# Leaving out TensorE weight loads whose tile the array already holds

## The chip, the cores and the metric

The kernel runs on one core of one Trainium2 chip. The metric is the device time of one execution in microseconds (us), lower is better. Most executions of one kernel agree within 0.3%; a change counts as faster or slower from 2% on.

## The reference

Four residual layers on an input of 2048 tokens by 1024 features in bf16: linear attention (A), gated MLP (B), A, B, each behind a layer norm. Cut to its arithmetic:

```python
def _A_ref(x, wqkv, wo):                       # 32 heads of 32
    q, k, v = split(x @ wqkv)
    pq, pk = phi(q), phi(k)                    # phi(t) = (t+1 if t>0 else exp(t)) + 1e-6
    kv = einsum("bhsd,bhse->bhde", pk, v);  z = sum_s(pk)
    o = (pq @ kv) / (pq . z + 1e-6)
    return o @ wo
def _B_ref(x, w_gate, w_up, w_down):           # F = 3584
    return ((x @ w_gate) * (x @ w_up)) @ w_down

x = x + _A_ref(ln(x)); x = x + _B_ref(ln(x)); x = x + _A_ref(ln(x)); x = x + _B_ref(ln(x))
```

## The kernel before

TensorE does nearly everything: its matmuls are busy 98% of the span. In the program a matmul names a stationary tile (128x128, the "weights" of the array, whether they come from a weight matrix or from activations) and the columns that go through it, 128 to 512 in this kernel. Each matmul is preceded by its own load of the stationary tile: the trace has 7,663 loads, all of 128x128. Two forms matter here.

The first is the helper for outputs of 1024 columns. It makes two matmuls of 512 columns with the **same** stationary tile, so every second load fetches a tile that is already there. The K, Q, G, M and output products of attention use it, and so does the down projection of the MLP:

```python
def both(ps, lhsT, rhs, start, stop):
    for n in range(2):
        nc.tensor.matmul(out=ps[:, n, :], lhsT=lhsT, rhs=rhs[:, n * NB:(n + 1) * NB], start=start, stop=stop)   # L205
...
def d_unit(t, last):                           # down projection of token tile t
    ...
    for f in range(KF):                        # KF = 28
        both(ps, hT[:, f, tl * P:(tl + 1) * P], wd[f], f == 0, f == KF - 1)
```

The second has a **new** stationary tile for every matmul: gate and up, and the small KV products of 128 columns:

```python
def gu_unit(i, f):
    ...
    for n in range(2):
        w = ring[(2 * i + n) % 6]
        for k in range(KD):                    # KD = 8
            nc.tensor.matmul(out=ps[:, n, :], lhsT=w[:, k, j * P:(j + 1) * P], rhs=xT[g % 2][:, k, :], ...)     # L437
def kv_unit(m):
    ...
    for c in range(KD):
        nc.tensor.matmul(out=acc[0][:, c, :], lhsT=wkv[:, m, c * P:(c + 1) * P],
                         rhs=Gs[m % 2][:, c * P:(c + 1) * P], ...)                                              # L295
```

The last token tile of the program (L464) has three passes of 512, 256 and 256 columns, again with a new tile each time.

## Time and profile before

| | before |
|---|---|
| time, median of the first 3 runs | 1659.09 us |
| span in the profile, granted TensorE clock | 1657.2 us, 0.995 of full |
| TensorE matmuls busy (PE) | 1627.2 us, 98% |
| weight loads (PEld), on a row of their own | 744.8 us, 45%, 7,663 loads |

The first lines of the page give the busy time of each engine with its share of the span and its instruction count:

```profile
span 1657.2 us, 17618 instructions
...
PE 1627.2 (98%) x7512; PEld 744.8 (45%) x7663; DVE 607.9 (37%) x889; ACT 286.3 (17%) x384; POOL 54.0 (3%) x141
...
q8 instruction: 60, 0.98, 0.2%
```

A busy share does not tell what limits TensorE, since records of neighbouring matmuls overlap: one of 512 columns lasts 379 ns but the next starts long before it ends. The *spacing* tells it. It is read in the chain of work that ended last, in order of time (columns: start in us, length in us, engine, output tile and line, number of matmuls). First the gate/up stage, then the down stage, then a KV product between two attention products:

```profile
272.53 10.74 PE ps L437 x49
283.27 0.05 issue
283.32 10.74 PE ps L437 x49
...
358.87 10.74 PE ps L205 x49
...
369.66 10.74 PE ps L205 x49
...
988.79 0.45 PE kv L295 x8
```

One matmul record in 50 is lost (gate/up has 3,513 matmul records beside 3,584 loads), which is why the pieces break; the 0.05 us is not a stall. A piece steps 10.79 us for 50 matmuls, 215.8 ns each, in both stages. In the last token tile a matmul of 512 columns steps 215.7 ns and one of 256 steps 109.3 ns, so 256 columns take 106.4 ns and 512 about 213 ns. The KV products step 0.45 us / 8 = 56 ns, each with a new tile. So TensorE streams columns almost without a break, and the 98 ns that a load record lasts lies beside the matmuls.

### The profile page before, as it was taken

To read this page: it belongs to the slowest core of one execution; us is meant where nothing else is said; L and a number is where in the kernel's file an instruction comes from. 1 tells how busy PE (TensorE), PEld (TensorE's weight loads), DVE (VectorE), ACT (ScalarE), POOL (GpSimd) and SP (SyncE) were. 2 spreads that over 40 slices of the span, in tenths; PEclk is the share of its full clock that TensorE was granted. 3 is DMA by queue.
4 is the path that set the end of the run, shared out by engine and by line. 5 is a ranking of instruction groups with operands and counts; after the bars stand their busy time and mean duration, and the time that the engine had idled before them with its cause. 6 is when DMAs were issued, how large, how long until landed. Compare 5 with 4: busy or idle time off the path is not lost.

```text
span 1657.2 us, 17618 instructions
## 1 busy us (share of the span) xinstructions
PE 1627.2 (98%) x7512; PEld 744.8 (45%) x7663; DVE 607.9 (37%) x889; ACT 286.3 (17%) x384; POOL 54.0 (3%) x141
## 2 busy tenths in 40 slices
PE   8989999999999999999999999999999999999999
PEld 3434444444444444444444444444444444444444
DVE  5797782311321231143345687532113113211111
ACT  4532301100110110011035322011001101100110
POOL 1100000000000000010000000000000000000000
PEclk9999999999999999999999999999999999999999
DMA  6322683630551363043420247555215504521400
GB/s 209 64 64 47 183 247 115 177 115 1 171 159 51 90 175 118 0 153 102 77 76 1 70 96 225 158 156 165 84 64 151 179 26 143 167 84 64 153 0 26
DMA packets 234686, 182.56 MB, mean 110 GB/s; under 512 B 100080, under 2 KB 215408, under 8 KB 234608
## 3 DMA queue, kind: packets, MB, share of 16 engines
q1 hardware_dynamic: 234608, 181.43, 37.5%
q8 instruction: 60, 0.98, 0.2%
q14 instruction: 18, 0.15, 0.0%
HBM read 153.09 MB, written 4.19 MB: 95 GB/s over the span
## 4 chain that ended last, share of the span: by engine, by line
PE 90%; DVE 7%; issue 1%; DMA 1%; POOL 1%; ACT 0%; SPq 0%; DVEq 0%; ACTq 0%
PE ps L437 46%; PE ps L205 42%; DVE GL L252 1%; DVE st L182 1%; PE ps L464 1%; DVE R L213 1%; DVE X L320 0%; DVE den L272 0%; DVE PQ L276 0%; PE kv L295 0%; POOL rstd L190 0%; DVE PQ L213 0%; DVE tmp L270 0%; DVE e L212 0%; DVE R L195 0%
## 5 line engine op out<-in xcount | busy, mean ns | idle before, releaser
L437 PE MATMUL ps<-xT,R 128*128 128x512 bf16 x2380 | 525.8, 379 | 2.8
L437 PEld LDWEIGHTS <-R 128*128 128x128 bf16 x2432 | 238.0, 98 | 287.0
L441 DVE TENSOR_TENSOR R<-gs,ps 128x512 bf16<-128x512 f32 x224 | 153.8, 687 | 533.6 <-ACT gs L440 533.6
L205 PEld LDWEIGHTS <-R 128*128 128x128 bf16 x2248 | 220.4, 98 | 266.6 <-issue 3.1
L440 ACT COPY gs<-ps 128x512 f32<-128x512 f32 x224 | 131.3, 586 | 1044.5 <-PE ps L437 1021.6
L437 PE MATMUL ps<-xT,W 128*128 128x512 bf16 x1133 | 250.6, 379 | 1.0
L205 PEld LDWEIGHTS <-xT 128*128 128x128 bf16 x1536 | 149.8, 98 | 184.2 <-issue 5.3
L205 PE MATMUL ps<-W,xT 128*128 128x512 bf16 x999 | 225.1, 380 | 4.5 <-ACT xT L345 1.7
L437 PEld LDWEIGHTS <-W 128*128 128x128 bf16 x1152 | 112.7, 98 | 135.9
L205 PE MATMUL ps<-W,R 128*128 128x512 bf16 x729 | 169.6, 379 | 0.7
L445 DVE TENSOR_TENSOR X<-X,ps 128x1024 bf16<-128x1024 bf16 (+2 forms) x34 | 39.4, 1158 | 335.9 <-PE ps L205 315.2
L205 PE MATMUL ps<-R,R 128*128 128x512 bf16 x503 | 114.5, 383 | 0.6
L205 PE MATMUL ps<-PQ,R 128*128 128x512 bf16 x484 | 111.5, 379 | 0.6
L205 PE MATMUL ps<-R,xT 128*128 128x512 bf16 x502 | 110.8, 379 | 0.9 <-DVE X L320 0.4
L210 ACT ACTIVATE e<-ps 128x1024 bf16<-128x1024 f32 x56 | 57.4, 1024 | 152.1 <-PE ps L205 150.6
L182 DVE BATCH_NORM_STATS2 st<-X 128x6 f32<-128x512 bf16 x128 | 82.1, 681 | 2.0 <-DMA X<-in_A_x_dram 1.8
L188 POOL TENSOR_SCALAR ve<-mv 128x1 f32<-128x1 f32 x64 | 15.7, 245 | 1362.8 <-DVE mv L186 1362.8
L205 PE MATMUL ps<-xT,R 128*128 128x512 bf16 x243 | 58.2, 379 | 0.3
L205 PE MATMUL ps<-GL,R 128*128 128x512 bf16 x244 | 58.2, 379 | 0.2
L320 DVE TENSOR_TENSOR X<-X,ps 128x1024 bf16<-128x1024 bf16 x32 | 38.5, 1209 | 33.1 <-PE ps L205 30.9
L212 DVE TENSOR_SCALAR e<-e 128x1024 bf16<-128x1024 bf16 x64 | 27.2, 424 | 63.2 <-ACT e L210 63.2
L195 DVE TENSOR_SCALAR R<-X,mv,rstd 128x1024 bf16<-128x1024 bf16 x64 | 33.7, 543 | 36.0 <-POOL rstd L190 36.0
(55 smaller groups left out, 462.9 us busy)
## 6 DMA issues: line engine op xcount, KB each, us to landing
R<-in_B_w_gate_dram SPq DMA_DIRECT2D x38, 1024.0 KB, 5.4
R<-in_B_w_up_dram SPq DMA_DIRECT2D x38, 1024.0 KB, 7.4
W<-in_B_w_gate_dram SPq DMA_DIRECT2D x18, 1024.0 KB, 5.2
W<-in_B_w_up_dram SPq DMA_DIRECT2D x18, 1024.0 KB, 7.2
W<-in_A_wqkv_dram SPq DMA_DIRECT2D x10, 1024.0 KB, 6.8
W<-in_B_w_down_dram SPq DMA_DIRECT2D x6, 1024.0 KB, 11.3
PQ<-in_B_w_down_dram SPq DMA_DIRECT2D x4, 1024.0 KB, 7.9
X<-in_A_x_dram SPq DMA_DIRECT2D x15, 256.0 KB, 5.7
```

What stands on the lines that cost most here:

```text
L182: nc.vector.bn_stats(out=st[:, c, :], in_=X[:, t, c * NB:(c + 1) * NB])
L195: nc.vector.tensor_scalar(out=dst, in0=X[:, t, :], scalar1=mv[:, 0:1], scalar2=rstd[:], op0=ALU.subtract, op1=ALU.mult)
L205: nc.tensor.matmul(out=ps[:, n, :], lhsT=lhsT, rhs=rhs[:, n * NB:(n + 1) * NB], start=start, stop=stop)
L210: nc.scalar.activation(out=e[:], in_=flat(ps), func=ACT.Exp, **sc)
L212: nc.vector.tensor_scalar(out=e[:], in0=e[:], scalar1=1.0, scalar2=EPS, op0=ALU.min, op1=ALU.add)
L213: nc.vector.tensor_tensor(out=dst, in0=dst, in1=e[:], op=ALU.add)
L252: nc.vector.tensor_tensor(out=zacc, in0=in0, in1=PK[:, t, :], op=ALU.add)
L320: nc.vector.tensor_tensor(out=X[:, t, :], in0=X[:, t, :], in1=flat(ps), op=ALU.add)
L437: nc.tensor.matmul(out=ps[:, n, :], lhsT=w[:, k, j * P:(j + 1) * P], rhs=xT[g % 2][:, k, :], start=(k == 0), stop=(k == KD - 1))
L440: nc.scalar.copy(out=gs[:], in_=ps[:, 0, :])
L441: nc.vector.tensor_tensor(out=hT[:, f, :], in0=gs[:], in1=ps[:, 1, :], op=ALU.mult)
L445: nc.vector.tensor_tensor(out=X[:, t, a:b], in0=X[:, t, a:b], in1=ps, op=ALU.add)
```

## The change

The intent: where two loads of the same tile follow one another, the second is useless; leaving it out takes a quarter of all loads away from TensorE. The program is compiled first, so that loads and matmuls are separate instructions and their waits are known. Then each load that names the tile of the load before it, and that carries no wait and no signal, is dropped.

```diff
+    ctx.close()
+    tc.close()
+    tc.compile()
+    for block in nc.cur_f.blocks:
+        held, keep = None, []
+        for i in block.instructions:
+            if isinstance(i, mybir.InstLdweights):
+                w = str(i.ins[0])
+                if w == held and not i.has_wait() and not i.has_update():
+                    continue
+                held = w
+            keep.append(i)
+        if len(keep) < len(block.instructions):
+            block.instructions[:] = keep
```

## The prediction

> **What bounds the kernel now.** The page shows TensorE busy 98% of a 1657.2 us span, clock 0.995; the chain that ended last is 90% TensorE matmuls, 7% VectorE. Matmul records overlap (379 ns each), so the spacing decides. In the chain in order of time, dense stages are equal pieces: 49 recorded matmuls end after 10.74 us and the next piece starts 10.79 us after this one, that is 50 matmuls (one record in 50 is lost) at 215.8 ns. [...]TensorE streams at nearly its peak; only about 40 us of the span are stalls and small matmuls.
>
> **Are weight loads visible in that spacing?** The 7,663 recorded loads take 744.8 us (45%), 98 ns each by the groups, but on their own row, under the matmuls. Gate/up (L437) needs a new tile for every matmul, the down stage (L205) repeats every second one: same piece, same step. The KV products (L295) run 8 matmuls of 128 columns, each with its own new load, in 0.45 us: 56 ns each, so even there the loads hide. In the last token tile (L464) the timeline gives 215.7 ns per 512 columns and 109.3 ns per 256: about 2.5 ns above the columns whatever the width. [...]
>
> **What the change removes.** Loads whose tile is already held and that carry no wait or signal. From the code: every second load of the two-half helper (K, Q, G, M, output and down projection), 1,908, 3 of 4 in each z sum (6), and 9 in the warm-up: about 1,923 of some 7,790. None in gate/up, KV products, transposes or last tile. At 98 ns that is 188 us of load time. It adds no instruction and moves no wait: matmuls, semaphores, DMAs stay.
>
> **On the critical path:** almost nothing. A kept load has at least one 213 ns matmul to hide under. In the attention stages with gaps the waits named are VectorE's, ScalarE's and DMA's, and the load after a wait is a first one, which stays. If the 2.5 ns belonged to the weight exchange, the gain would be at most 1,914 x 2.5 = 4.8 us (0.3%). I give that a quarter: about -1 us.
>
> **Predicted time:** 1657.5 us, range 1652 to 1661. Faster by over 2%: 0.01; within 2%: 0.96; slower by over 2%: 0.03.
>
> **What would show it.** Recorded loads fall to about 5,740, their busy time to about 560 us (34%); matmul count, 379 ns and busy share stay. The step of 50 matmuls in the down stage stays 10.79 us if the 2.5 ns are the matmul's own, and becomes about 10.73 if the repeated load carries them. Gate/up must not move. Attention stalls stay.
>
> **What would make it wrong.** If the load for the next tile could start only after the second matmul of a pair, each pair would lose up to 98 ns: 188 us slower, seen as gaps before first matmuls. If repeated loads cost more than the spacing shows, it would be faster, but by no more than the distance to pure streaming, under 1% outside the stalls. The clock at 0.995 leaves nothing to gain.

The forecast's one term is a quarter of 4.8 us, about -1 us, and it comes to 1657.5 us. The "columns" and the "peak" in it are those of the 213 ns that the steps above give.

## The result

| | before | after |
|---|---|---|
| time, median (range), 6 runs each | 1658.74 us (1657.57 to 1659.62) | 1657.98 us (1657.17 to 1659.35) |
| ratio | | 0.9997, 95% interval 0.9985 to 1.001 |
| span and clock of the profiled run | 1657.2 us, 0.995 | 1656.8 us, 0.995 |

A ratio here and below is the mean time of one kernel's fast runs over that of the other's of the same rounds, so not quite the ratio of the medians quoted. Part of the spread goes with the clock: the six runs after the change fall into three near 1657.3 us with clock 0.996 and three near 1659.0 us with 0.995, and 0.1% of 1657 us is 1.7 us. Against that spread the 0.8 us between the medians means nothing.

The page after the change:

```profile
span 1656.8 us, 15695 instructions
...
PE 1626.9 (98%) x7512; PEld 556.8 (34%) x5740; DVE 607.8 (37%) x889; ACT 286.3 (17%) x384; POOL 54.0 (3%) x141
...
q8 instruction: 52, 0.85, 0.2%
```

1,923 loads are gone, and with them 188 us of load busy time; the matmuls are as busy as before. The chain after, same stages:

```profile
272.03 10.74 PE ps L437 x49
...
282.82 10.74 PE ps L437 x49
...
358.37 10.74 PE ps L205 x49
...
369.16 10.74 PE ps L205 x49
...
988.29 0.45 PE kv L295 x8
```

The step of 50 matmuls is 10.79 us in gate/up, which lost no load, and 10.79 us in the down stage, which lost half of them. The gain was not made there and given back later: in the stages concerned it was never there. The groups of loads (columns: line, engine, operation, tile, count, busy us, mean ns of one, idle us before them and what ended it) show which went. Before:

```profile
L437 PEld LDWEIGHTS <-R 128*128 128x128 bf16 x2432 | 238.0, 98 | 287.0
L205 PEld LDWEIGHTS <-R 128*128 128x128 bf16 x2248 | 220.4, 98 | 266.6 <-issue 3.1
```

After:

```profile
L437 PEld LDWEIGHTS <-R 128*128 128x128 bf16 x2432 | 238.0, 98 | 288.2 <-issue 2.0
L205 PEld LDWEIGHTS <-R 128*128 128x128 bf16 x1124 | 110.2, 98 | 376.3 <-issue 374.4 <-DVE GL L252 0.3 <-DVE e L212 0.3
```

The load row turned busy time into idle time, one for one. The attention stalls did not move either: the longest named wait of a matmul, for the summed z that VectorE writes, is 6.7 us in total (twice, 5.1 us the longer) in both profiles.

### The profile page after: what moved, and what is told of

It is laid out like the page before. It is cut to its first block, busy times and chain, and to the rows that moved or that the text cites. A ratio compares the mean times of both kernels' runs of the same rounds, so it can differ in the third digit from the quotient of the medians.

```text
span 1656.8 us, 15695 instructions
## 1 busy us (share of the span) xinstructions
PE 1626.9 (98%) x7512; PEld 556.8 (34%) x5740; DVE 607.8 (37%) x889; ACT 286.3 (17%) x384; POOL 54.0 (3%) x141
## 4 chain that ended last, share of the span: by engine, by line
PE 90%; DVE 7%; issue 1%; POOL 1%; ACT 0%; DMA 0%; SPq 0%; DVEq 0%; ACTq 0%
PE ps L437 46%; PE ps L205 43%; DVE GL L252 1%; DVE st L182 1%; PE ps L464 1%; DVE R L213 1%; DVE X L320 1%; DVE den L272 0%; DVE PQ L276 0%; PE kv L295 0%; POOL rstd L190 0%; DVE PQ L213 0%; DVE tmp L270 0%; DVE e L212 0%; DVE R L195 0%
## 5 line engine op out<-in xcount | busy, mean ns | idle before, releaser
L437 PEld LDWEIGHTS <-R 128*128 128x128 bf16 x2432 | 238.0, 98 | 288.2 <-issue 2.0
L205 PEld LDWEIGHTS <-R 128*128 128x128 bf16 x1124 | 110.2, 98 | 376.3 <-issue 374.4
L205 PEld LDWEIGHTS <-xT 128*128 128x128 bf16 x768 | 75.4, 98 | 254.3 <-issue 246.4
L212 DVE TENSOR_SCALAR e<-e 128x1024 bf16<-128x1024 bf16 x64 | 27.2, 424 | 63.0 <-ACT e L210 63.0
```

Source lines behind the costliest of these rows:

```text
L212: nc.vector.tensor_scalar(out=e[:], in0=e[:], scalar1=1.0, scalar2=EPS, op0=ALU.min, op1=ALU.add)
```

## The experiments

My theory (A): a load lies wholly beside the matmul that runs before it, and the 2.5 ns that a matmul takes above its columns is the matmul's own, so no saving of loads can show in this kernel. Rivals: (B) the 2.5 ns is the exchange of the tile; (C) something was saved and given back; (D, E) the loads only just fit, so the slack is thin; and later some about what a load costs once it is no longer hidden. The first two experiments were timed in five rounds, the two with narrow matmuls in three; the others had one look each, are of unknown state, and are read by the steps in their traces.

### Nearly all loads left out

Edit to the loop of the change: any load without wait or signal is dropped if the array holds *some* tile of the same mode. Its output is wrong, which doesn't matter for the time.

```diff
-                w = str(i.ins[0])
+                w = (str(i.is_transpose), str(i.perf_mode))
                 if w == held and not i.has_wait() and not i.has_update():
```

> All weight loads without a wait or signal are left out wherever the array holds some tile of the same mode: about 205 of 7,663 load rows are left, and the result is wrong on purpose. It bounds what any saving of loads can give. Theory A (loads lie wholly under the matmuls, the 2.5 ns above the columns is the matmul's own): 1655 to 1659 us, no change in the dense stages, 50 matmuls still step 10.79 us. Rival B (the 2.5 ns is the exchange of the tile and shows only where a new tile comes in, which the pairs could have masked): 7,460 x 2.5 ns = 18.6 us less, about 1640 us, 50 matmuls in 10.67 us. Rival C (the saving was real and was given back in the attention stages): shorter dense stages and longer waits for VectorE there.

Measured: 1658.53 us (5 runs, 1655.02 to 1659.31) against 1659.03 us of before; ratio 0.9994, interval 0.9982 to 1.0007. First the line of the page:

```profile
PE 1626.7 (98%) x7512; PEld 20.1 (1%) x205; DVE 607.9 (37%) x889; ACT 286.3 (17%) x384; POOL 53.9 (3%) x141
```

and the chain in gate/up:

```profile
272.07 10.74 PE ps L437 x49
...
282.86 10.74 PE ps L437 x49
```

With 205 of 7,663 loads left, the load row goes from 45% to 1% and 50 matmuls still step 10.79 us. Rival B wanted 10.67 us and about 1640 us; it falls. The 2.5 ns is there with hardly any loads. Rival C wanted shorter dense stages; it falls too. This bounds the whole idea: in this kernel all weight loads together cost nothing that can be measured, so a quarter of them could not be worth anything.

### Every load doubled

```diff
             keep.append(i)
+            if isinstance(i, mybir.InstLdweights):
+                keep.append(copy_of(i))      # same tile, new name, no wait or signal; no load is dropped
```

> Every load is issued twice in a row; the result stays right. Theory A with a load that occupies the array port for 56 ns or less (the KV products bound it): 2 x 56 = 112 ns fit under 213 ns, the time stays within 1 us or so of before, 1657 to 1660 us, load busy share near 90%. Only the KV products get slower, 128 x 56 ns at most, 7 us. Rival D (the slack is thin: a load occupies the port for its whole 98 ns): 2 x 98 = 196 ns still just fit; KV products 128 x 140 ns = 18 us slower at most. Rival E (a second load [...]can't start until the running matmul ends): about 98 ns more per matmul, some 700 us slower.

Measured: 1658.12 us (5 runs, 1655.87 to 1659.64), correct; ratio to before 0.9994, interval 0.9981 to 1.0008. First the line of the page:

```profile
PE 1626.1 (98%) x7512; PEld 1038.5 (63%) x15326; DVE 608.0 (37%) x889; ACT 286.3 (17%) x384; POOL 53.9 (3%) x141
```

and the chain in the down stage and at a KV product:

```profile
358.88 10.74 PE ps L205 x49
...
369.67 10.74 PE ps L205 x49
...
988.88 0.46 PE kv L295 x8
```

7,663 more loads leave the step at 10.79 us; rival E falls. Even the KV products, 56 ns apart, take 0.46 us for 8 instead of 0.45. My own numbers were off here: I had expected a load row near 90% and up to 7 us on the KV products; it is 63%, since records of neighbouring loads overlap (15,326 of 97 ns would add up to 1,487 us), and the KV products barely moved.

### A ladder of loads

How much slack is there? In the first MLP layer's down stage, each 512-column matmul gets more loads of its tile, by group of four token tiles.

```diff
-                both(ps, hT[:, f, tl * P:(tl + 1) * P], wd[f], f == 0, f == KF - 1)
+                for n in range(2):
+                    for _ in range(0 if last else (1, 2, 3, 5)[t // TPG]):
+                        nc.tensor.ldweights(hT[:, f, tl * P:(tl + 1) * P])
+                    nc.tensor.matmul(out=ps[:, n, :], lhsT=hT[:, f, tl * P:(tl + 1) * P],
+                                     rhs=wd[f][:, n * NB:(n + 1) * NB], start=(f == 0), stop=(f == KF - 1))
```

> In the down stage of the first MLP layer each matmul has 2, 3, 4 or 6 loads of its own tile (token tiles 0-3, 4-7, 8-11, 12-15). The result stays right. Theory A with 56 ns or less per load: step per matmul 215.8 ns with 2 and 3 loads, about 224 or less with 4, about 336 or less with 6; the slope between 4 and 6 gives the true cost of a load. Rival D (98 ns each): 216, 294, 392, 588 ns. Rival E[...]: already about 310 ns with 2.

Measured: 1659.63 us (one run), correct. The chain with 4 loads per matmul, then with 6:

```profile
661.42 10.74 PE ps L457 x49
...
672.21 10.74 PE ps L457 x49
...
790.92 10.78 PE ps L457 x49
...
801.76 10.78 PE ps L457 x49
```

With 2, 3 and 4 loads the step is 215.8 ns; with 6 it is 10.84 us / 50 = 216.7 ns. Theory A had only given upper bounds, 224 ns with 4 loads and 336 ns with 6, and they hold with much room; rival D wanted 392 and 588 ns. Six loads fit, within 1 ns, where the kernel has one, so the slack is large and rival D falls.

### Narrow matmuls, with all loads and with the change

If the loads hide under the columns, they should show where the columns are few. Both down stages use 256, 128, 64 and 32 columns by group of token tiles. In the first MLP layer the matmuls of one tile follow one another, so the change can take all loads but one per tile; in the last, each matmul has a new tile (the control).

```diff
+            wid = (256, 128, 64, 32)[t // TPG]
+            steps = [(f, c) for f in range(KF) for c in range(D // wid)]
+            if last:
+                steps = [(f, c) for c in range(D // wid) for f in range(KF)]
+            for f, c in steps:
+                nc.tensor.matmul(out=flat(ps)[:, c * wid:(c + 1) * wid], lhsT=hT[:, f, tl * P:(tl + 1) * P],
+                                 rhs=wd[f][:, c * wid:(c + 1) * wid], ...)
```

With all loads:

> The down stages use matmuls of 256, 128, 64 and 32 columns in token tiles 0-3, 4-7, 8-11 and 12-15, each with its load; in the first MLP layer matmuls that share a tile follow one another, in the last one each has a new tile. The result stays right. Theory A: 109 ns at 256 and 56 ns at 128 (columns plus 2.5 ns), and below that the load shows: step of 64 and 32 columns stays at the load's own cost, somewhere from 30 to 56 ns. Rival F (issue of instructions is the limit for small matmuls, each load and each matmul costing one slot, and the 8 KV products were only quick because they had queued up): at 128 columns already more than 56 ns with loads, and the same at 64 and 32 columns. Both layers alike, if loads of a held tile cost what others do.

With the change on top:

> The same as the run with narrow matmuls, with the change on top: in the first MLP layer one load serves 4, 8, 16 or 32 matmuls, in the last one all loads stay (the control). Theory A: no gain at 256 and 128 columns, 29 ns at 64 columns and 25 ns or less at 32, against the load's cost before: a clear gain only there. Rival F: the step at 128, 64 and 32 columns halves at most, as the number of instructions does. The last layer must not move.

Measured: 1778.52 us (4 runs, 1776.12 to 1782.33) with all loads, 1755.53 us (4 runs, 1753.48 to 1758.3) with the change, both correct; before, on the same chip, 1657.08 us. The ratios to before are 1.0735 (1.0715 to 1.0755) and 1.0591 (1.0576 to 1.0607). The steps in the first MLP layer, from the chains, each the mean of a group with its pauses:

| columns | all loads | with the change |
|---|---|---|
| 256 | 109.2 ns | 109.2 ns |
| 128 | 55.8 ns | 55.8 ns |
| 64 | 31.4 ns | 29.2 ns |
| 32 | 29.5 ns | 25.0 ns |

The chain with all loads: the whole 128-column group, the start of the 64-column group, and the start and the longest pause of the 32-column group:

```profile
498.96 50.03 PE ps L458 x896
...
645.68 6.21 PE ps L458 x213
651.89 2.26 issue
...
798.60 6.89 PE ps L458 x276
...
805.57 3.35 PE ps L458 x128
808.92 0.65 issue
809.57 3.35 PE ps L458 x128
...
890.63 3.41 issue
```

The same with the change, where each of the groups is one unbroken piece:

```profile
500.03 50.03 PE ps L458 x896
...
646.75 52.27 PE ps L458 x1792
...
795.71 89.59 PE ps L458 x3584
```

The steps are near what theory A expected: no gain at 256 and 128 columns, 29 and 25 ns with the change below. So the change saves time only there: (56.2 - 52.3) + (105.8 - 89.6) = 20 us in these two groups; the two profiled spans differ by 18.2 us, and the medians by 23.0. The control stays within its pauses: in the last layer's 32-column group, where each matmul has a new tile, three token tiles take 77.5 and 76.5 us. A new tile is no dearer than a repeated one (about 29 ns per matmul there, 29.5 here).

Theory A expected a load's own cost to show as an even step. That is not what the trace has. The first 276 matmuls of the 32-column group, each with its load, take 6.89 us, 25.0 ns each, as without loads. After them come pauses after *every 128 pairs*, that is after 256 instructions: 0.1 to 0.7 us in the chain, and once 3.4 us. Between the pauses the matmuls still start 25.0 ns apart: 3,421 of the 3,576 steps in the trace are that, and 128 more are 26 to 27 ns. (The 3.35 us of a piece of 128 include the last record, 0.176 us long, so the step is 3.17 us / 127, not 3.35 / 128.) At 64 columns nearly the whole difference is one pause of 2.26 us and 63 matmuls soon after it that step 53 ns; the stretch from 655 to 658 us shows a granted clock of 0.51. The other steps there are 29 to 30 ns, as without loads. So no load's own cost shows even here. The instruction queue (q8 of the pages) has the same distance: from the run with 205 loads to the one with 15,326 it goes from 31 packets of 0.51 MB in all to 90 of 1.47 MB, which is 15,121 / 59 = 256 instructions and about 16 KB for each further packet. So the next theory (A2) is that what shows first is the supply of instructions: a load is paid for as an instruction, not as a load. Rival F, a fixed slot per instruction from 128 columns on, falls with the 55.8 ns.

### How many loads per narrow matmul before it shows

The whole down stage of the first MLP layer at 32 columns, with the held tile loaded again never, before every fourth, every second, and every matmul, by group of token tiles. The loop of the change was given a keep-every number by group:

```diff
+            if b - a == 32:                             # a run of 32 loads of one tile
+                every = (32, 4, 2, 1)[n // (TPG * KF)]
+                n += 1
+            drop |= {i.name for j, i in enumerate(loads[a:b]) if j % every and not i.has_wait() and not i.has_update()}
```

> All four token groups of the first MLP layer's down stage use 32-column matmuls; a held tile is loaded again never, before every fourth, before every second, before every matmul. Theory A2 (supply of instructions, 14.6 ns each, against 25.0 ns of matmul): 25.0 ns per matmul for the first three (1.03, 1.25 and 1.5 instructions per matmul need 15, 18 and 22 ns), without gaps, and about 29.5 ns in the fourth, with gaps every 256 instructions. Rival G' (each load costs the array a few ns by itself, 29.5 - 25.0 = 4.5): 25.1, 26.1, 27.2 and 29.5 ns, a straight line in the number of loads, no gaps in the first three.

Measured: 1838.15 us (one run), correct. The chain: two groups whole, the third, and the start of the fourth:

```profile
353.68 89.59 PE ps L455 x3584
...
539.97 89.59 PE ps L455 x3584
...
726.27 5.57 PE ps L455 x223
731.83 0.29 issue
732.12 84.18 PE ps L455 x3361
...
913.00 8.94 PE ps L455 x358
...
922.00 3.35 PE ps L455 x128
925.35 0.67 issue
```

The first two groups take 89.59 us, 25.0 ns per matmul, although the second has eight times the loads of the first. The third, one load for two matmuls, takes 90.0 us with a single gap of 0.3 us. The fourth runs its first 358 matmuls at 25.0 ns with a load each, then has the gaps again, and takes 28.9 ns per matmul in all. Rival G', a few ns for each load, wanted 26.1 and 27.2 ns in the second and third group; it falls. The 25 blocks of 256 instructions from 922.00 to 1015.90 us took 3.76 us each, 14.7 ns per instruction: 1.5 instructions per matmul need 22 ns and hide under 25.0, two need 29.4 ns and don't. That fits A2 in all four groups. What stays open: I could not feed instructions other than loads at the same rate as a control. That the load itself costs nothing here is shown by the 25.0 ns between the gaps. That the gaps are the supply of instructions is argued from where they fall and from the threshold, not shown by a filler, and what made some of them longer was not tested.

### The ladder higher up

The ladder with 8, 12, 16 and 24 loads per 512-column matmul:

```diff
-                    for _ in range(0 if last else (1, 2, 3, 5)[t // TPG]):
+                    for _ in range(0 if last else (7, 11, 15, 23)[t // TPG]):
```

> The ladder of loads higher up: 8, 12, 16 and 24 loads of the tile before each 512-column matmul of the first MLP layer's down stage (token tiles 0-3, 4-7, 8-11, 12-15). Theory A2 (a load takes the array at most about 26 ns, the step of 32-column matmuls with loads, and really less; what shows first is the supply of instructions, 256 of which took about 3.74 us in the run with narrow matmuls, gaps counted, so 14.6 ns each): 216 ns with 8 and 12, about 17 x 14.6 = 248 with 16, about 25 x 14.6 = 366 with 24, in bursts with gaps of issue every 256 instructions. Rival G (the load itself takes 26 ns of the array): 216, 312, 416, 624 ns, evenly. Rival D (98 ns each) is 784 ns with 8.

Measured: 2043.02 us (one run), correct, mean clock 0.899. All my expectations missed. The chain with 8 loads (the whole group), 12 loads and 16 loads:

```profile
353.38 66.45 PE ps L457 x224
...
517.05 0.39 PE ps L457
...
517.50 0.39 PE ps L457
...
723.84 0.61 PE ps L457
...
724.57 0.61 PE ps L457
```

8 loads give 66.45 us / 224 = 296.6 ns per matmul, 12 give 457 ns, both at full clock: 40.0 ns for each further load, evenly, so step = 40.0 ns x loads - 23.4 ns. That line gives 216.6 ns for 6 loads, and the first ladder had 216.7. It gives 616.6 ns for 16 loads, and the first twelve steps of that group, from 715.74 to 723.14 us and still at full clock, are 616.7 ns. After them the stretches with 16 and 24 loads show a clock of 0.50, although the load row is full (busy 40.00 of 40 us), and the steps are 727 and 1,100 ns. So loads did not keep the clock up. By the line, columns run for 47% of a step with 12 loads, where the clock stayed at 1.00, and for 35% with 16; where between them it turns, and whether this share decides it, no run shows. A load in a row of loads costs 40.0 ns, more than twice the 14.7 ns per instruction of the run before, while a single load before each matmul costs nothing of its own even where the matmuls are 25.0 ns apart. Rival G had the right shape, with 26 ns in place of 40.

### A narrow ladder

Does the 40 ns depend on the matmul that runs beside it? The ladder with 128-column matmuls and 1, 2, 3 and 5 loads each:

```diff
+            wid = NB if last else 128
+            for f, c in [(f, c) for f in range(KF) for c in range(D // wid)]:
+                for _ in range(0 if last else (0, 1, 2, 4)[t // TPG]):
+                    nc.tensor.ldweights(hT[:, f, tl * P:(tl + 1) * P])
+                nc.tensor.matmul(...)
```

> 128-column matmuls in the first MLP layer's down stage with 1, 2, 3 and 5 loads of the tile before each (token tiles 0-3, 4-7, 8-11, 12-15). From the two ladders with 512 columns, step = 40.0 ns x loads - 23.4 ns, once that is above the matmul's own step. Theory H (loads in a row cost 40 ns each whatever the matmul's width, and the matmul's columns run beside them): 55.8, 56.6, 96.6 and 176.6 ns per matmul while the clock is full. Rival I (loads hide only under the matmul's columns and the 512-column matmul hid the rest): with 2 loads the narrow matmul shows them already, 80 to 95 ns, and about 135 ns with 3. If the granted clock falls to 0.5 in the last group, its step is longer, as in the ladder's high end.

Measured: 1848.2 us (one run), correct. The chain with two loads (the whole group, one pause of 0.32 us in it) and with three:

```profile
500.03 8.26 PE ps L457 x143
...
508.61 47.83 PE ps L457 x753
...
653.20 86.57 PE ps L457 x896
```

Whole groups in the chain give 50.03 us / 896 = 55.8 ns with one load, about 63 ns with two (57.8 before the pause, 63.5 after it), and 86.57 us / 896 = 96.6 ns with three; with five it is 212 ns, nearly all of it at a clock of 0.50. Theory H had 55.8, 56.6, 96.6 and, at full clock, 176.6 ns: exact for three loads, 6 ns short for two, at the knee. The first 36 steps with five loads, before the clock fell, are 177 ns, as it said. Rival I wanted 80 to 95 ns with two loads and 135 with three; it falls. Why the second load of a pair costs what the first does not is not settled: the runs give the line, not its mechanism.

## Why the prediction was right

- **"TensorE streams at nearly its peak"**, read from the step of 215.8 ns against 213.3 ns of columns: right. Removing 97% of all loads moved neither step nor time, so no load was in that step. What the 2.5 ns are was not asked further.
- **"Loads hide"**: right, and by more than I knew. I had only the bound of 56 ns from the KV products. The ladder shows room for five more loads beside each 512-column matmul.
- **"About 1,923" loads removed, 5,740 left, 556 to 560 us busy**: measured 1,923, 5,740 and 556.8 us. By group the counts drop from 2248 to 1124, 1536 to 768, 32 to 16, 8 to 2 and 11 to 2. One slip: I wrote of "some 7,790" loads issued; the program has 7,663, as recorded. Matmul records get lost in the trace of before (7,512 are left; the run with 8 to 24 loads, with as many matmuls, has 7,663), load records do not.
- **"If the 2.5 ns belonged to the weight exchange" (given a quarter, -1 us)**: it does not. The down stage stays at 10.79 us per 50, also with almost no loads left. The 0.8 us between the medians is not that term but spread. That the forecast of 1657.5 us, which counted it in, came within 0.5 us of the measured median is luck: the six runs spread over 2 us.
- **What would have made it wrong**, a load that could start only after the second matmul of a pair: no sign of it; the pairs step as before.

The prediction argued from the spacing in stages with and without repeated tiles. That comparison could show that loads hide, but not whose the 2.5 ns is, because both stages had one load per matmul. Only leaving the loads out could tell that.

## What to carry to other kernels

Judge a weight load by the step from matmul to matmul, not by its own busy time: 745 us of load time cost nothing here, because each load ran beside the matmul before it. The busy share of loads was 1%, 34%, 45% and 63% in four kernels whose times agree within 0.1%. Leaving out repeated loads pays only where matmuls are so narrow (32 columns here; at 64 it was a single pause and a dip of the clock) that TensorE, as it seems, runs out of instructions (14.7 ns each there), or where several loads stand in a row (40.0 ns for each further one with 8 and 12 per 512-column matmul). If that is the case, wider matmuls are the better cure: the narrow kernel with the change was still 6% slower than the wide one without it (ratio 1.0591). Before building such a change, take the whole suspected cost away, even at the price of a wrong result, and see whether the time moves.
